# A long convolution factored 256 x 16 or 64 x 64: what the layout of the spectral stages does to the time of a two-head kernel

## The chip, the core and the metric

The kernel runs on one core of a Trainium2 chip. A core has TensorE (PE, with its weight loads as PEld), VectorE (DVE), ScalarE (ACT), GpSimd (POOL) and SyncE (SP), each with an instruction stream of its own that runs in program order, and sixteen DMA engines that move data between HBM and SBUF. SP and POOL issue the DMAs of this kernel: SP on the queue that the profile calls q1, POOL on q0. The metric is the device time of one execution in microseconds; the median of several runs counts. A profile is taken of one execution, and its span goes from the first to the last instruction.

## The reference

Two heads share nothing but the output tensor. With S = 2048 positions and D = 1024 channels:

```python
# head A: short shift filter, gate, long causal convolution by FFT of length 4096, gate
k_shift = sum(k_pad[:, t:t + S, :] * shift_k[:, ks - 1 - t] for t in range(4))
kv = k_shift * v
y  = irfft(rfft(pad(kv, 2 * S)) * rfft(pad(ssm_k, 2 * S)))[:S]
a  = q * (y + kv * ssm_D)
# head B: diagonal complex state space
Lam_bar = exp(dt * Lam);  B_bar = ((Lam_bar - 1) / Lam)[:, None] * Bmat
Bu = einsum("bld,pd->blp", x, B_bar)
h  = scan over t of  Lam_bar * h + Bu[:, t]
b  = 2 * einsum("blp,dp->bld", h, Cmat).real + x * Dskip
out = concatenate([a, b], axis=-1)       # (1, 2048, 2048), bf16
```

## The kernel before

**Head A** computes the length-4096 transform in two factors, N1 = 256 by N2 = 16, with odd frequencies, so that 128 complex values of k1 are enough. Position n is split as n = 16 n1 + n2, n1 on the 128 partitions and n2 from 0 to 15.

- *kv* (L539 to L575): `kp` and `vp` load two n2 rows of k and v for all 128 n1, `kvm`, `kva`, `kvb`, `kvc` build kv for one n2 on DVE.
- *First stage* (L577 to L589): `am` multiplies the kv of one n2 by the 128 x 128 cosine or sine matrix `F1t`, one matmul of 128 x 512 for each of two halves of D and two parts; `ae` evicts the PSUM bank on ACT; `ast` stores 256 KB to the DRAM scratch `Ys_kv` from POOL. `hl`, `hT`, `hc`, `hm`, `he`, `hst` (L591 to L633) do the same for the filter `ssm_k`, after a transpose on PE, into `Ys_h`.
- *Second stage* (L635 to L689), for 16 groups gq of two k1 per partition block: `lh` and `lk` load `Ys_h` and `Ys_kv` again, now with (part, n2, k1 block) on the partitions (512 KB each, SP); `sh` and `sk` multiply by the group's weights `wts` (loaded by `lw`), two matmuls with 64 output rows each that lie in the two halves of one bank; `she` and `ske` evict; `pr` forms the two products on DVE; `sa` transforms back, two matmuls with 64 input rows each into two banks; `sae` evicts and `vst` stores 512 KB to the scratch `Vs`.
- *Third stage* (L691 to L718): `vl` loads both parts of one n2 from `Vs` (two SP loads of 256 KB), `a3` multiplies by `Gt` (two accumulating matmuls of 128 x 512 per half of D), `a3e` evicts, `qm` multiplies by q (loaded by `qp`), `ost` stores to the output from POOL.

There are two barriers in the data: a second-stage group needs all of `Ys_h` and `Ys_kv`, and a third-stage load needs all of `Vs`.

**Head B** fills the engines beside it. For each of 16 chunks of 128 positions: `x` loads x transposed, `U` (L461, 16 matmuls of 128 columns per half step) gives the input projections, `ue` evicts, `r1`, `r2`, `rc`, `sc`, `cm`, `ca`, `r3`, `r4` rotate, scan and rotate back on DVE, `y` (L517) does the output projection, `ye` evicts, `yst` stores. The set-up loads, transposes and tables (`bl`, `bT`, `bc`, `cl`, `cT`, `cc`, `cx`, `tab...`) come first.

**The order.** Everything is issued in the order of one long string, `ORDER`, fixed in the source: each word is a task with its indices, and behind a colon the buffers that it takes (`p` PSUM banks, `a` 4 KB slots, `b` 2 KB slots, `m`, `w`). The framework adds the semaphores that data and buffer reuse need. An engine runs its own instructions in that order, so a DMA on SP or POOL that waits holds up those behind it. `spd` is a DMA issued by SP, `gpd` one issued by POOL.

The lines that matter for a transfer are those that say how DRAM is walked, for instance

```python
kr = k.rearrange("(n s) d -> n s d", s=N2)                                    # 128 x 16 x 1024
Ys.rearrange("c n (s g) d -> (c n s) g d", g=NG)[:, gq * GC:(gq + 1) * GC, :] # l2: 128 x (2 x 1024)
spd(st["vv", n2][:, cc, :], Vs[cc, n2, :, :])                                 # vl: 128 x 1024
```

Of the kernel before, what the change touches and what calls it, by code (L numbers as in the profile page):

```python
# [21 lines left out]
N1, N2, NFFT = 256, 16, 4096  # L22
NG = 32


def a_constants():
    n1 = np.arange(128)[:, None]; k1 = np.arange(128)[None, :]
    ang = 2 * np.pi * n1 * (k1 + 0.5) / N1
    F1 = np.stack([np.cos(ang), -np.sin(ang)], axis=1)
    G = np.stack([np.cos(ang.T) * 2 / NFFT, -np.sin(ang.T) * 2 / NFFT], axis=1)  # L30
    s = np.arange(4)[:, None, None, None]; g = np.arange(NG)[None, :, None, None]
    n2 = np.arange(N2)[None, None, :, None]; k2 = np.arange(N2)[None, None, None, :]
    kk1 = 32 * s + g
    phi = 2 * np.pi * n2 * (2 * kk1 + 1 + 2 * N1 * k2) / (2 * NFFT)
    cph, sph = np.cos(phi), np.sin(phi)
    W2 = np.zeros((2, 4, N2, NG, 2, 4, N2))
    Wa = np.zeros((2, 4, N2, NG, 2, 4, N2))
    Wb = np.zeros((2, 4, N2, NG, 2, 4, N2))
    for si in range(4):
        c_ = cph[si]; s_ = sph[si]  # L40
        c_n2k2 = np.transpose(c_, (1, 0, 2)); s_n2k2 = np.transpose(s_, (1, 0, 2))
        W2[0, si, :, :, 0, si, :] = c_n2k2
        W2[1, si, :, :, 0, si, :] = s_n2k2
        W2[0, si, :, :, 1, si, :] = -s_n2k2
        W2[1, si, :, :, 1, si, :] = c_n2k2
# [12 lines left out]
    Wb = np.transpose(Wb, (0, 1, 2, 3, 4, 6, 5))
    wa = Wa.reshape(2, 64, NG, 128)[0]
    wb = Wb.reshape(2, 64, NG, 128)[0]  # L60
    half = lambda a: np.transpose(a.reshape(64, NG // 2, 2, 128), (2, 0, 1, 3)).reshape(128, NG // 2, 1, 128)
    W3 = np.concatenate([W2.reshape(128, NG // 2, 2, 128), half(wa), half(-wa), half(wb)], axis=2)
    return f(F1), f(G), f(W3)

# [3 lines left out]

ORDER = """
ld_w:a0a1 wb.3:p0 wb.2:p1 wb.0:p2 wb.1:p3 wbe.1 bl.3.1:b0 wb.7:p4 bl.3.0:b1 ld_par par_T:p5 p32 exp1 dve2 exp2 wbe.3 dve3 wbe.2 wb.4:p6 wbe.4  # L70
bl.2.1:b2 bT.2.1:p3 sm_pre bT.3.0:p5 bc.3.0 tabA1:a0a2a3a4 sin0 wbe.7 bl.4.0:b3 bT.4.0:p0 bc.4.0 bl.0.1:b4 bl.2.0:b5 bl.1.0:b6 bT.2.0:p6 wb.5:p5
bc.2.0 bT.3.1:p1 bT.0.1:p4 bl.0.0:b7 bT.0.0:p7 bc.0.0 bc.2.1 sin1 bT.1.0:p0 x.3:b8 U.3.1.0:p3 wb.6:p6 bc.3.1 U.3.1.1 bl.1.1:b9 bT.1.1:p7 bc.0.1 wbe.5
bc.1.0 wbe.6 x.1:b10 U.1.0.0:a1p5 tabA2 wbe.0 U.1.1.0:p0 U.1.1.1 x.2:b2 U.2.1.0:p2 bc.1.1 U.3.0.0:a5p7 ue.3.1 U.2.0.0:a6p3 U.2.0.1 sin2 par_rest eo
kp.1 U.2.1.1 ue.2.1 ue.2.0 z1 kp.0 dd kvm.3:m0 bl.5.0:b0 cl.2.0:b4 bT.5.0:p6 kva.3 kvb.3:b9 bc.5.0 x.0:b5 U.0.0.0:a7p4 U.0.0.1 bl.7.1:b6 U.0.1.0:p3
U.0.1.1 bl.4.1:b7 bT.4.1:p2 U.1.0.1 stt bc.4.1 ue.0.0 kp.-1 bl.5.1:b3 U.3.0.1 ue.3.0 bl.6.0:b1 ue.1.0 kvm.1:m0 cl.2.1:b11 bT.6.0:p2 bT.5.1:p4 bc.5.1
bc.6.0 U.0.2.0:p6 kva.1 kvb.1:b3 z2 cT.2.1:p5 bT.7.1:p7 bc.7.1 bl.6.1:b12 bT.6.1:p4 bc.6.1 kp.-2 kvm.0:m1 kva.0 kvb.0:b12 U.0.2.1 bl.7.0:b13 vp.0:a8
cT.2.0:p2 kvc.1 U.3.2.0:p1 cl.1.0:b14 bT.7.0:p7 U.3.2.1 bc.7.0 vp.1:a9 ue.1.1 ue.0.1 U.1.3.0:p4 U.1.3.1 U.0.3.0:p3 ue.0.2 ue.1.3 kvc.0 ld_F am.0.0:p6
cl.1.1:b0 ae.0.0:b13 U.0.3.1 ue.0.3 kvm.2:m1 cT.1.0:p4 cc.1.0 r1.0:m0 am.0.2:p6 cl.3.1:b7 cT.3.1:p0 x.4:b1 cc.3.1 ae.0.2:b7 cT.1.1:p3 cc.1.1
U.4.0.0:a8p7 cc.2.1 cl.3.0:b11 U.3.3.0:p4 U.3.3.1 ue.3.3 cT.3.0:p6 kva.2 kvb.2:b0 U.4.0.1 kvc.2 ue.4.0 cl.0.0:b6 cT.0.0:p5 cc.0.0 r2.0:a7 cl.0.1:b4
cc.2.0 sc.0.0 am.1.2:p4 am.0.1:p3 U.1.2.0:p0 ae.1.2:b6 U.1.2.1 ae.0.1 cT.0.1:p5 cc.3.0 am.1.3:p2 ast.0.0 sc.0.1 cm.0 ae.1.3 ast.1.1 r3.0:m0 r4.0  # L80
am.0.3:p7 ae.0.3 ast.0.1 U.2.2.0:p4 U.2.2.1 cc.0.1 ue.1.2 am.2.0:p2 r1.1:m1 r2.1:a0 ae.2.0:b12 U.4.3.0:p6 cx.7.0 hl.1.0:a4 U.4.3.1 ue.4.3 hl.0.0:a2
hl.0.1:a3 hT.0.0:p0 hc.0.0:b4 hl.1.1:a10 hT.1.3:p2 hT.1.0:p5 hc.1.0:b13 ld_sd hd.0 am.1.0:p6 ue.3.2 ae.1.0:b6 am.1.1:p7 ae.1.1 am.2.1:p3 ast.1.0
ae.2.1 hd.1 U.2.3.0:p0 hc.1.3:b7 hT.0.2:p5 hc.0.2:b3 U.4.2.0:p1 U.4.2.1 ue.4.2 U.2.3.1 hm.0.0.2:p2 he.0.0.2:b11 x.5:b14 U.5.0.0:a1p3 hm.0.0.3:p1
he.0.0.3 kvc.3 ca.0 rc.1 lw.2:w0 sc.1.0 hm.0.0.0:p5 he.0.0.0:b6 sc.1.1 y.0.0.0:p2 y.0.0.1 U.5.0.1 ast.2.0 hst.0.0.1 cm.1 hm.0.0.1:p5 ue.2.2 ue.2.3
r1.2:m1 hm.0.2.0:p4 cx.5.1 lw.1:w1 hm.1.0.0:p0 he.1.0.0:b4 he.0.0.1 r3.1:m0 am.2.2:p1 ae.2.2:b12 cx.4.1 am.2.3:p7 ae.2.3 y.0.0.2 y.0.0.3 hm.0.2.2:p1
hm.1.0.1:p5 cx.6.0 U.5.3.0:p7 hm.1.3.2:p0 r2.2:a6 ca.1 ast.2.1 he.1.0.1 hst.1.0.0 rc.2 hst.0.0.0 hm.1.0.3:p5 he.0.2.0:b11 hm.0.2.3:p6 hm.0.2.1:p4
he.0.2.2:b0 he.0.2.3 hst.0.2.1 U.5.3.1 r4.1 he.0.2.1 r1.3:m1 ue.5.3 sc.2.0 sc.2.1 cm.2 hT.0.3:p6 ca.2 hm.1.0.2:p4 U.5.2.0:p1 ue.5.0 he.1.3.2:b3
hT.1.2:p3 he.1.0.2:b13 r2.3:a5 rc.3 hm.1.3.0:p0 he.1.3.0:b12 he.1.0.3 hm.1.3.1:p7 he.1.3.1 y.1.0.0:p4 kp.3 hT.1.1:p0 hc.1.1:b4 hst.1.0.1 cx.6.1
hc.0.3:b6 U.5.1.0:p5 U.5.1.1 hm.1.1.3:p0 ue.5.1 cx.4.0 cx.5.0 cx.7.1 y.1.1.0:p7 hm.1.1.2:p5 ye.0.0:b0 hm.1.3.3:p6 he.1.3.3 hst.1.3.1 y.1.0.1
he.1.1.2:b7 he.1.1.3 lw.0:w2 hst.1.1.1 kp.2 kvm.4:m0 hT.0.1:p2 hc.0.1:b13 hc.1.2:b3 y.0.1.0:p6 hm.0.3.2:p0 y.0.1.1 hst.0.2.0 hm.1.1.0:p2 he.1.1.0:b5  # L90
y.0.1.2 hst.1.3.0 y.0.1.3 ye.0.1 hm.0.3.3:p5 he.0.3.2:b7 y.1.0.2 U.5.2.1 y.1.0.3 sc.3.0 ue.5.2 hl.2.1:a9 hm.0.3.0:p2 hm.0.3.1:p6 he.0.3.0:b6 kva.4
hm.1.1.1:p3 he.1.1.1 y.1.1.1 hl.2.0:a4 hT.2.3:p2 hT.2.0:p3 yst.0 he.0.3.3 he.0.3.1 hst.0.3.0 hc.2.0:b12 hm.1.2.3:p5 hm.1.2.2:p1 hst.1.1.0 he.1.2.2:b10
he.1.2.3 r3.2:m1 ye.1.0:b4 y.1.1.2 y.1.1.3 ye.1.1 U.4.1.0:p1 yst.1 U.4.1.1 hc.2.3:b0 hst.1.2.1 hm.0.1.0:p7 sc.3.1 cm.3 hst.0.3.1 ca.3 vp.4:a10 hd.2
hm.2.0.3:p4 hm.2.0.2:p2 hm.2.3.0:p5 he.2.3.0:b11 he.2.0.2:b6 he.2.0.3 hst.2.0.1 hl.3.0:a2 r4.2 y.2.0.0:p3 y.2.0.1 r3.3:m1 r4.3 hm.2.0.0:p2 he.2.0.0:b5
hm.2.3.2:p4 vp.2:a3 kvm.5:m1 hm.1.2.0:p5 hm.2.3.1:p6 he.2.3.1 hm.2.0.1:p0 he.2.0.1 kvb.4:b10 y.2.0.2 he.1.2.0:b12 ue.4.1 y.2.0.3 am.3.0:p0 ae.3.0:b4
kvm.6:m0 kva.6 hst.2.3.0 hm.0.1.1:p5 hm.1.2.1:p6 he.1.2.1 am.3.1:p1 he.0.1.0:b7 he.0.1.1 he.2.3.2:b3 hst.2.0.0 hst.0.1.0 hl.3.1:a7 hT.3.0:p2
y.2.1.0:p0 y.2.1.1 y.2.1.2 hc.3.0:b6 hst.1.2.0 am.3.2:p2 kvc.4 ae.3.1 ast.3.0 ye.2.0:b2 hd.3 hm.0.1.2:p4 hm.2.3.3:p1 hm.0.1.3:p5 he.0.1.2:b11 he.0.1.3
am.3.3:p7 y.2.1.3 am.4.3:p4 am.4.2:p5 ae.4.2:b5 ae.4.3 y.3.0.0:p3 y.3.0.1 ast.4.1 ae.3.2:b9 ae.3.3 ast.3.1 hm.3.0.2:p4 kvb.6:b0 hm.3.0.0:p2 ye.2.1
he.2.3.3 hst.2.3.1 kva.5 am.4.0:p5 ae.4.0:b12 kvb.5:b13 am.4.1:p7 kvc.5 yst.2 vp.3:a0 kvc.6 am.6.2:p6 hst.0.1.1 he.3.0.2:b10 ae.4.1 hm.3.0.3:p0
# [77 lines left out]
ye.14.1 yst.14 a3.7.1:p1 a3e.7.1 ost.11 vl.1:a16 qm.7 ost.7 ost.5 qp.6:a10 a3e.12.0:b12 a3e.12.1 qm.12 ost.12 a3.1.1:p4 a3.1.0:p7 a3.0.1:p2  # L177
a3e.1.0:b13 a3.0.0:p1 a3e.0.0:b0 vl.6:a3 y.15.1.0:p3 a3.6.1:p7 ost.3 a3e.4.1 qm.15 ost.15 qp.0:a14 a3.6.0:p5 qm.4 y.15.1.1 a3.13.1:p6 a3e.6.0:b1
a3e.6.1 y.15.0.0:p5 y.15.0.1 ost.4 y.15.0.2 y.15.0.3 qm.6 ost.6 y.15.1.2 a3e.9.1 qm.9 a3e.1.1 a3e.0.1 qm.0 ost.0 qm.1 ost.1 a3e.13.1 qm.13 ost.13
y.15.1.3 ye.15.0:b12 ost.9 ye.15.1 yst.15  # L180
"""


def full_kernel(ctx, tc, A_q, A_k, A_v, A_shift_k, A_ssm_k, A_ssm_D, B_x, B_Lre, B_Lim, B_Bre, B_Bim,
# [600 lines left out]
```

## Time and profile before

| | |
|---|---|
| median of 3 runs | 389.83 us (389.46 to 393.08) |
| the profiled execution | 391.46 us |
| its span | 389.7 us |
| granted TensorE clock | 0.992 |
| DMA traffic | 92.49 MB, mean 237 GB/s |
| HBM read, written | 52.05 MB, 33.55 MB |
| first stage: `am` L580, `hm` L619 | 64 matmuls of 512 columns, 128 of 256 |
| third stage: `a3` L706 | 64 matmuls of 512 columns |
| `hst` on POOL, L632 | 64 issues, 46.1 us |

How to read it: busy time of PE is the union of its matmuls, which are pipelined, so one that takes 379 ns from start to end may start 216 ns after the one before. A share of the DMA engines is a mean over sixteen. A landing time goes from the issue to the last semaphore update of a transfer, so it includes time in the queue. In the view of stages the columns are the stretch, its length, busy time of each engine with the number of instructions, the granted clock, the DMA share and GB/s.

### The profile page before, as it was taken

The page shows a single profiled execution, that of the slowest core. Times are in us where ns is not written, and L with a number is a line of the kernel's source. Part 1 is how long each engine was busy: PE and PEld are TensorE (multiplying, and loading weights), DVE is VectorE, ACT ScalarE, POOL GpSimd, SP SyncE. Part 2 cuts the span into 40 slices and gives each one's busy share as a digit, 9 for nine tenths or more (in the row PEclk, how much of TensorE's full clock was granted, in tenths as well). Part 3 has the DMA queues.
Part 4 walks back from the last instruction along what each step waited for, and adds up shares of the span by engine and source line. Part 5 has one row for each costly group of instructions (what it writes and reads, how often), then busy time and mean ns, then how long its engine had stood idle before and what let it go on. Part 6 is the DMA issues. An engine that isn't in the chain of part 4 may idle for free.

```text
span 389.7 us, 9237 instructions
## 1 busy us (share of the span) xinstructions
PE 363.3 (93%) x3785; PEld 244.9 (63%) x3785; DVE 332.3 (85%) x335; ACT 278.1 (71%) x519; POOL 93.0 (24%) x156
## 2 busy tenths in 40 slices
PE   4899996999998997999999999999999999999990
PEld 2799995866655866888564556644564656564440
DVE  3899997998899999599999999897897996397760
ACT  3999896767697675869498876887889690345560
POOL 2000022554865652634000002011000320002260
PEclk9999999999999999999999999999999999999996
DMA  8999999676878699586856569748674828879782
GB/s 231 276 301 316 296 181 250 200 228 234 278 205 318 211 238 226 163 274 219 280 204 212 126 208 283 255 145 280 200 275 150 334 109 277 286 252 307 267 319 80
DMA packets 56005, 92.49 MB, mean 237 GB/s; under 512 B 30078, under 2 KB 32126, under 8 KB 55964
## 3 DMA queue, kind: packets, MB, share of 16 engines
q1 hardware_dynamic: 45308, 58.21, 52.9%
q0 software_dynamic: 10656, 33.71, 24.0%
q8 instruction: 29, 0.48, 0.5%
q14 instruction: 12, 0.10, 0.1%
HBM read 52.05 MB, written 33.55 MB: 220 GB/s over the span
## 4 chain that ended last, share of the span: by engine, by line
PE 51%; ACT 14%; issue 12%; DVE 10%; DMA 9%; POOL 2%; POOLq 0%; ACTq 0%; DVEq 0%
PE ps_y L524 18%; PE ps_u L469 15%; PE ps_a L680 4%; PE ps_a L650 4%; DMA Ys_h<-ysbh 4%; ACT hh L657 3%; PE ps_a L619 3%; PE ps_a L580 3%; ACT xx L663 3%; DVE mt L560 2%; DMA Ys_kv<-ysb 2%; ACT vsb L687 2%; DMA out_dram<-ot 2%; DVE mt L567 2%; POOL out_dram L718 1%
## 5 line engine op out<-in xcount | busy, mean ns | idle before, releaser
L524 PE MATMUL ps_y<-CT,h 128*128 128x512 bf16 x512 | 127.0, 379 | 0.3 <-ACT ot L712 0.2
L469 PE MATMUL ps_u<-xT,BT 128*128 128x128 bf16 x2048 | 124.7, 219 | 0.6 <-ACT BT L445 0.3
L469 PEld LDWEIGHTS <-BT 128*128 128x128 bf16 x2048 | 118.4, 98 | 10.5 <-issue 4.1
L524 PEld LDWEIGHTS <-h 128*128 128x128 bf16 x512 | 45.2, 98 | 45.0 <-issue 2.4
L500 DVE TENSOR_TENSOR_SCAN h<-rtab,h 128x1024 bf16<-128x1024 f32 x32 | 71.9, 2279 | 0.3
L471 ACT CAST u<-ps_u 128x512 bf16<-128x512 f32 x64 | 38.6, 628 | 33.0 <-PE ps_u L469 24.4
L632 POOL DMA_DIRECT2D Ys_h<-ysbh x64 | 46.1, 722 | 29.0 <-ACT ysbh L625 23.3
L625 ACT CAST ysbh<-ps_a 128x512 bf16<-128x512 f32 x64 | 35.6, 616 | 16.9 <-PE ps_a L619 6.6
L481 DVE TENSOR_TENSOR mt<-u,Z 128x4096 bf16<-128x4096 bf16 x16 | 36.5, 2281 | 9.6 <-ACT u L471 9.6
L587 ACT CAST ysb<-ps_a 128x512 bf16<-128x512 f32 x64 | 35.5, 630 | 8.2 <-PE ps_a L580 4.1
L689 POOL DMA_DIRECT2D Vs<-vsb x16 | 8.5, 534 | 122.8 <-ACT vsb L687 96.7
L657 ACT CAST hh<-ps_a 128x512 bf16<-128x512 f32 x64 | 36.0, 649 | 2.3 <-PE ps_a L650 2.2
L589 POOL DMA_DIRECT2D Ys_kv<-ysb x32 | 17.5, 551 | 81.4 <-ACT ysb L587 81.4
L481 DVE TENSOR_TENSOR mt<-h,Z 128x4096 bf16<-128x4096 bf16 x16 | 36.6, 2287 | 0.2
L687 ACT CAST vsb<-ps_a 128x512 bf16<-128x512 f32 x64 | 34.2, 694 | 3.3 <-PE ps_a L680 3.3
L663 ACT CAST xx<-ps_a 128x512 bf16<-128x512 f32 x64 | 35.8, 660 | 0.6 <-PE ps_a L650 0.6
L535 ACT CAST yo<-ps_y 128x512 bf16<-128x512 f32 x32 | 19.5, 626 | 16.4 <-PE ps_y L524 16.3
L560 DVE TENSOR_TENSOR mt<-kring,wbc 128x4096 bf16<-128x4096 bf16 (+3 forms) x16 | 30.1, 1884 | 0.1
L529 PE MATMUL ps_y<-Dd,xT 128*128 128x128 bf16 x128 | 28.0, 219 | 0.0
L619 PE MATMUL ps_a<-hT,F1t 128*128 128x256 bf16 x128 | 20.5, 272 | 5.6 <-ACT hT L607 3.6
L712 ACT CAST ot<-ps_a 128x512 bf16<-128x512 f32 x32 | 17.4, 606 | 10.7 <-PE ps_a L706 6.3
L670 DVE TENSOR_TENSOR pp<-xx,hh 128x2048 bf16<-128x2048 bf16 x16 | 19.4, 1220 | 6.0 <-ACT xx L663 3.5
(110 smaller groups left out, 460.3 us busy)
## 6 DMA issues: line engine op xcount, KB each, us to landing
Ys_kv<-ysb POOLq DMA_DIRECT2D x32, 256.0 KB, 3.6
Ys_h<-ysbh POOLq DMA_DIRECT2D x64, 128.0 KB, 3.5
l2h<-Ys_h SPq DMA_DIRECT2D x16, 512.0 KB, 5.7
l2k<-Ys_kv SPq DMA_DIRECT2D x16, 512.0 KB, 4.6
Vs<-vsb POOLq DMA_DIRECT2D x16, 512.0 KB, 5.4
vv<-Vs SPq DMA_DIRECT2D x32, 256.0 KB, 4.9
kring<-in_A_k_dram SPq DMA_DIRECT2D x8, 512.0 KB, 4.3
v<-in_A_v_dram SPq DMA_DIRECT2D x8, 512.0 KB, 5.9
```

The lines of the kernel that those rows point to most:

```text
L469: nc.tensor.matmul(pu[:, w, jl, :], BT[:, 2 * jp + jl, w, d, :], xT[:, d, :], start=(d == 0), stop=(d == ND - 1))
L471: E["ue"] = lambda i, jp: nc.scalar.copy(st["u", i][:, :, 2 * jp:2 * jp + 2, :], st["pu", i, jp][:])
L481: nc.vector.tensor_mul(m, s_, win(Z))
L500: nc.vector.tensor_tensor_scan(gf, rt1, gf, 0.0, ALU.mult, ALU.add)
L524: nc.tensor.matmul(py[:], h[:, 1 - w, j, :], CT[:, j, w, dh * 512:(dh + 1) * 512], start=(j == 0 and w == 0), stop=(j == NJ - 1 and w == 1))
L560: nc.vector.tensor_mul(m[:, 0:h0, :], kring[:, s0:s0 + h0, :], wbc[:, 0:h0, :])
L587: nc.scalar.copy(st["ysb", n2, cc][:, dh * 512:(dh + 1) * 512], st["pa", n2, w][:])
L625: nc.scalar.copy(st["yh", qd, n4, w // 2][:, :, w % 2, :], st["pa", qd, n4, w][:].rearrange("p (c d) -> p c d", c=2))
L632: gpd(Ys_h[cc, n0:n0 + 2, :, qd * DQ:(qd + 1) * DQ].rearrange("n k d -> k n d"), t_[:, cc, :, :])
L657: nc.scalar.copy(st["hh", gq][:, cc, w * 512:(w + 1) * 512], st["ps", "l2h", gq, cc, w][:])
L663: nc.scalar.copy(st["xx", gq, cc][:, w * 512:(w + 1) * 512], st["ps", "l2k", gq, cc, w][:])
L687: nc.scalar.copy(st["vsb", gq][:, gi, w * 512:(w + 1) * 512], st["ps", "v", gq, w][gi][:])
```

## The change

The transform is factored N1 = 64 by N2 = 64 instead of 256 by 16, so that 32 complex values of k1 (HK) are enough. Position n is now split as n = 64 n1 + 16 q + s, with q from 0 to 3 and s from 0 to 15 (NB): a tile of k, v or q has (q, n1) on its 128 partitions.

- The first kv stage needs matrices of 32 x 64 (`F1t`), the last one of 64 x 32 (`Gt`). A new helper `pieces` places eight such matmuls at different rows and columns of the array, each with 512 columns, into four banks (`am`, for two s at once) or two banks (`a3`, for two n2 at once).
- The filter's first stage uses a block-diagonal matrix `Fht` of the full 128 x 128, one matmul of 512 columns in place of two of 256; `hst` becomes one store of 256 KB in place of two of 128 KB.
- The second stage keeps its matmuls and evictions, with dense weights. `l2` issues two loads of 256 KB per tensor and group in place of one of 512 KB.
- The scratch tensors change their layout, and with them every DRAM pattern of `ast`, `hst`, `l2`, `vst` and `vl`; k, v, q and the output of head A are walked as `q n s d`.
- Twelve stores, nine `ost` and three `yst`, are issued by SP instead of POOL.
- `ORDER` is a new string with new slots; the constants get one more load (`ld_H`).

```diff
-N1, N2, NFFT = 256, 16, 4096
-NG = 32
+N1, N2, NFFT = 64, 64, 4096
+HK = N1 // 2
+NB = 16
...
+SP_STORES = frozenset("ost.0 ost.4 ost.5 ost.6 ost.7 ost.8 ost.9 ost.12 ost.13 yst.11 yst.12 yst.15".split())
+    stq = lambda kind, n: spd if "%s.%d" % (kind, n) in SP_STORES else gpd
...
-    Ys_kv = tc.dram_tile([2, N2, P, D], BF16, name="Ys_kv")
-    Ys_h = tc.dram_tile([2, N2, P, D], BF16, name="Ys_h")
-    Vs = tc.dram_tile([2, N2, P, D], BF16, name="Vs")
-    kr = k.rearrange("(n s) d -> n s d", s=N2)
...
+    Ys_kv = tc.dram_tile([4, HK, 2, NB, D], BF16, name="Ys_kv")
+    Ys_h = tc.dram_tile([4, HK, 2, NB, D], BF16, name="Ys_h")
+    Vs = tc.dram_tile([HK, 2, N2, D], BF16, name="Vs")
+    kr, vr, qr, oar = (a_.rearrange("(n q s) d -> q n s d", q=4, s=NB) for a_ in (k, v, q, out_a))
...
     def kp(r):
         if r >= 0:
-            spd(t_, kr[:, 2 * r:2 * r + 2, :])
+            spd(t_, kr[:, :, 2 * r:2 * r + 2, :])
         else:
-            spd(t_[1:113, :, :], kr[0:112, N2 + 2 * r:N2 + 2 * r + 2, :])
-            spd(t_[113:P, :, :], kr[112:P - 1, N2 + 2 * r:N2 + 2 * r + 2, :])
+            rows = slice(NB + 2 * r, NB + 2 * r + 2)
+            spd(t_[32:P, :, :], kr[0:3, :, rows, :])
+            spd(t_[1:32, :, :], kr[3, 0:31, rows, :])
...
+    def pieces(banks, rows, weights, cols):
+        m = weights.shape[-1]
+        for r, pt in enumerate(banks):
+            rs = slice(rows * r, rows * r + rows)
+            for j in range(P // m):
+                nc.tensor.matmul(pt[m * j:m * j + m, :], weights[rs, :], cols(j, r)[rs], start=True, stop=True)
+
+    def am(u, w):
+        st["pa", u, w] = [ptile("ps_a", [P, 512]) for _ in range(4)]
+        pieces(st["pa", u, w], 32, F1t[:], lambda j, r: st["kv", 2 * u + j][:, w * 512:(w + 1) * 512])
...
+    def ast(u, r):
+        gpd(Ys_kv[r, :, :, 2 * u:2 * u + 2, :].rearrange("k c t d -> t (k c) d"), st["ysb", u, r][:])
...
     def hm(qd, n4, w):
-        for cc in range(2):
-            nc.tensor.matmul(pt[:, cc * DQ:(cc + 1) * DQ], F1t[:, cc, :], st["hT", qd, n4][:, w, :], start=True, stop=True)
+        nc.tensor.matmul(pt[:], Fht[:, qp_, :], st["hT", qd, n4][:, 2 * tp:2 * tp + 2, :].rearrange("p a b -> p (a b)"), start=True, stop=True)
...
+    def hst(qd, n4, qp_):
+        dst = Ys_h.rearrange("(b q) k c t d -> b (q k c) t d", b=2)
+        gpd(dst[qp_, :, 4 * n4:4 * n4 + 4, qd * DQ:(qd + 1) * DQ], st["yh", qd, n4, qp_][:])
...
     def l2(nm, Ys, gq):
-        spd(st[nm, gq][:], Ys.rearrange("c n (s g) d -> (c n s) g d", g=NG)[:, gq * GC:(gq + 1) * GC, :])
+        for gi in range(GC):
+            spd(st[nm, gq][:, gi, :], Ys[:, gq * GC + gi, :, :, :].rearrange("q c t d -> q (c t) d"))
...
+    E["vst"] = lambda gq: gpd(Vs[gq * GC:(gq + 1) * GC].rearrange("g c n d -> (c n) g d"), st["vsb", gq][:])
+
+    def vl(u, h):
+        st["vv", u, h] = k4("vv", [P, 2, D])
+        src = Vs.rearrange("k c (q t) d -> t (k c) q d", q=4)
+        for a in range(2):
+            spd(st["vv", u, h][:, a, :], src[2 * u:2 * u + 2, :, 2 * h + a, :])
...
+    def a3_(u, w):
+        st["po", u, w] = [ptile("ps_a", [P, 512]) for _ in range(2)]
+        pieces(st["po", u, w], 64, Gt[:], lambda j, r: st["vv", u, j // 2][:, j % 2, w * 512:(w + 1) * 512])
...
-    E["ost"] = lambda n2: gpd(oar[:, n2, :], st["ot", n2][:])
+    E["ost"] = lambda n2: stq("ost", n2)(oar[:, :, n2, :], st["ot", n2][:])
```

## The prediction

> **What bounds the kernel now.** I read the page's part 1 first, then busy time by stage. The stages are cut where the trace cuts them: the last store of Ys_kv starts at 183.2 us and the first load of l2k at 187.0; the last store of Vs starts at 320.4 and the first load of vv, which needs every Vs store, at 323.6.
>
> ```profile
> PE 363.3 (93%) x3785; PEld 244.9 (63%) x3785; DVE 332.3 (85%) x335; ACT 278.1 (71%) x519; POOL 93.0 (24%) x156
> ```
> ```profile
> core 0: us, PE busy (x) PEld busy (x) DVE busy (x) ACT busy (x) POOL busy (x), PEclk, DMA share, GB/s
> 0.00:185.00 185.00, 169.72 (x2113) 136.22 (x2115) 165.79 (x199) 143.50 (x254) 69.49 (x112) 1.00 0.87 244
> 185.00:317.00 132.00, 131.03 (x1214) 73.85 (x1213) 122.50 (x97) 106.19 (x213) 10.09 (x19) 1.00 0.66 218
> 317.00:381.00 64.00, 62.58 (x464) 34.85 (x459) 44.03 (x41) 28.43 (x55) 12.89 (x25) 1.00 0.81 283
> 381.00:390.00 9.00, 0.00 (x0) 0.00 (x0) 0.00 (x0) 0.00 (x0) 0.54 (x1) 0.64 0.11 43
> ```
>
> PE is busy 131.0 of 132 us in stage B and 62.6 of 64 in stage C; in A and B DVE is nearly as full. PE and DVE set the pace, and transfers are hidden. But the DMA share, a mean over 16 engines, is already 0.66 to 0.87: there is no room for a transfer that uses few of the sixteen. So the last views are the DMA issues and the landings (the first landing line is that of vv, the second of l2k).
>
> ```profile
> DMA packets 56005, 92.49 MB, mean 237 GB/s; under 512 B 30078, under 2 KB 32126, under 8 KB 55964
> q1 hardware_dynamic: 45308, 58.21, 52.9%
> q0 software_dynamic: 10656, 33.71, 24.0%
> l2h<-Ys_h SPq DMA_DIRECT2D x16, 512.0 KB, 5.7
> l2k<-Ys_kv SPq DMA_DIRECT2D x16, 512.0 KB, 4.6
> vv<-Vs SPq DMA_DIRECT2D x32, 256.0 KB, 4.9
> ```
> ```profile
> DMA to landing us min/median/max: 2.6/4.9/5.6
> DMA to landing us min/median/max: 3.4/4.6/7.9
> ```
>
> **The compute side of the change.** Three answers price it: the timeline of PE around old two-piece stages and around `a3`.
>
> ```profile
> 229.63 0.59 PE L680 MATMUL ps_a<-pp,wts 64*128 64x512 bf16 x4
> 230.06 0.60 PE L680 MATMUL ps_a<-hh,wts 64*128 64x512 bf16 x4
> 368.08 3.62 PE L706 MATMUL ps_a<-vv,Gt 128*128 128x512 bf16 x16
> ```
>
> Sixteen whole-array matmuls take 3.62 us; less the latency of one (0.38), 15 steps of 0.216. Four half-array ones start 0.43 us before the next four: two run beside each other. At 207.85 an L524 follows four L680 that start at 207.31, 0.54 later and not 0.43: a change of array shape costs 0.1 us.
>
> - `am` and `a3`: 128 matmuls of 0.216 (27.6 us) become 32 groups of eight. Eight at once: 0.216 and up to two shape changes, 0.22 to 0.42 a group, 7 to 13 us, a gain of 15 to 21. One after another: 256 x 0.216 = 55.3, a loss of 28. I take 17 gained, by the nearest row (two pieces do run beside each other).
> - `hm`: 128 of 256 columns become 64 of 512, the same columns: nothing. Evictions stay 128x512 in the same number: nothing on ACT. DVE's work is unchanged.
> - POOL: `hst` falls from 64 to 32 issues, 46.1 us of POOL busy to perhaps 30. POOL is 24% busy: nothing. SP gets 32 more l2 issues and 12 stores, 44 x 0.38 = 17 us; it mostly waits. A store on SP waits for `qm` or `ye`, and behind it wait the `vl` and `qp` loads, 0 to 2 us each late in stage C; I count nothing, since the transfers' own time below is longer.
> - Tail: POOL's drain at L780 starts at 381.2 with the last store and takes 7.65 us; the span ends at 389.7. After, POOL's last stores are `yst.14` and `ost.11`, before `yst.15` is done; 0 to 4 us gained.
> - Order and slots: counts per engine and stage stay, apart from some U and y moved into stage C; 5 us either way.
>
> Alone these give about 389.7 - 17 - 2 = 371, bounded by DVE's 332 us of work and some 17 of start and tail (349).
>
> **The transfers.** Every large copy of before has 128 rows as outermost count on both sides. The change permutes DRAM: `kr, vr, qr, oar` read "q n s d", counts 4 x 32 x row; l2 reads `q (c t) d`, 4 x 32 x 1,024; `vl` reads `t (k c) d`, 2 x 64 x 1,024. The two `kp` loads with negative index become 3 x 32 rows and 31 rows.
>
> How a copy is cut over engines can be read from the trace's packet records. Each engine that takes part in a copy on q1 ends with a 4-byte packet. There are 144 plain copies and 24 transposing ones (32 such packets each, 768). If all used sixteen engines there would be 3,072; there are 3,038. The 34 missing are exactly 4 x 8 for the parameter loads of 8 rows and 2 x 1 for the `kring` loads of 15 rows. So a copy is divided over as many engines, up to sixteen, as its outermost count gives. q0 (POOL) posts sixteen for each of its 149 copies, and shows nothing of this. I extend the row to the new shapes: 4 engines for kp, vp, qp, l2 and `ost` on SP, 2 for `vl`, 3 and 1 for the odd `kp`, always the first ones, since no record shows a rotation. That is the step that carries the forecast.
>
> The Trainium skill says the same against this change: "DMA: Bandwidth & Descriptors", section "Why a DMA increments its semaphore by 16 and not by 1", has the issuer take the largest number up to 16 that divides the slowest dimension of both sides, on hardware queues the lowest-numbered engines. By it the sum stays as below; the trace agrees in the 34 packets, and no run yet shows it for a pattern that is 4 or 2 on the DRAM side alone.
>
> What one engine moves: in the records a 2,048-byte packet on q1 takes 84 ns (median), 24.4 GB/s. Ends: vv against l2k, 256 KB more cost 0.8 us on sixteen engines, 20.5 GB/s each; a 4,096-byte packet at 156 ns at least is 26.3 GB/s. I take 84 ns, since the new loads are rows of 2 KB.
>
> Load of engine 0, by stage:
> - A: 16 kp and vp of 512 KB, 64 packets of 2 KB each: 1,024 x 84 ns = 86 us. Odd kp: 2 x (64 + 62) x 84 = 21. The rest stays spread: 0.87 x 185 = 161, less the old k and v (9.4 MB / 16 / 24.4 = 24) = 137. Together 244; but packets overlap (the share reaches 1.13 in 10 to 40 us), and at 26 GB/s it is some 195. Between: 210.
> - B: 64 l2 loads x 32 x 84 ns = 172. Rest: 0.66 x 132 = 87, less old l2 (16.8 MB / 16 / 24.4 = 43) = 44. Three `qp`: 16. Three early `lh` fall in A: -16. Sum 216; with a few idle us at the start of the stage 220.
> - C: `vl` 32 x 64 x 84 ns = 172. All of them come after the last Vs store. Five `qp` 27, nine `ost` on SP 24, rest about 15: 238.
> - Tail 8.
>
> 210 + 220 + 238 + 8 = **676 us** of span. The profiled execution took 391.46, 1.8 beyond its span, and the median of the runs is 1.6 below it; the two cancel, and I say 675. PE's gain vanishes: in C it has some 50 us of work (9 half-U of 0.9, 40 y parts of about 0.92, a3 5).
>
> Stores on POOL with counts 2 and 4 (`ast`, seven `ost`): if they too sat on the first engines, `ast` would add 172 us to A; spread, nothing. I take nothing, since q0 posts on all sixteen.
>
> Ends: at 20.5 GB/s A 245, B 268, C 284, together with the tail 800; at 26.3 GB/s 190, 195, 208, together 600. A mixed case decides the range's ends, 590 to 790.
>
> **Rivals.**
> 1. *The SBUF side's 128 partitions decide the cut* (faster). Then all sixteen engines serve, vv lands in 3 to 5 us as now, and the compute sum holds: about 372. It decides from seven engines up: the `vl` loads take 344/k us on k engines, and at k = 7 they pass under stage C's 50 us of PE work. For it: only copies that are short on both sides show fewer engines so far. Against: nothing in the rows says that one side is exempt. 0.10.
> 2. *Few engines, but others each time.* Bytes spread; only landing grows, for vl 1.9 + 64 x 84 ns = 7.3 us. Prefetch hides most: 372 to 395, say 385. 0.05.
> 3. *The pieces run one after another* with loads as in 1: 389.7 + 28 - 2 of tail = about 416, as PE has no idle time to take it in. Against: the pairs above. 0.03.
>
> **How the numbers follow.** Forecast 0.82, range 590 to 790 nearly all of it, so close to 0.8 in all. Faster by over 1%: rival 1 and part of 2, 0.12; within 1% 0.01; slower 0.87. One per cent is about what a measurement of this kernel can tell from no change.
>
> **What would show it.** Right: stage C some 240 us long with traffic near 75 GB/s in place of 283; vv to landing tens of us, and `a3` waiting for DMA vv; fewer q1 packets of 4 bytes than copies times sixteen; in B, L650 waiting for l2h and l2k. The pieces: eight L706-like starts within some 0.1 us. Wrong: vv landing near 5 us and PE still over 90% busy. The forecast also fails in size if an engine moves far more than 26 GB/s, or if PE's clock falls in the waits so far that compute matters again.

## The result, and the profile after

The changed kernel takes **729.57 us** (725.6 to 730.67, four runs) against 391.01 us (389.46 to 393.08, four runs) of the kernel before, timed beside it: 1.863 times as long, interval 1.851 to 1.876. The profiled execution took 730.67 us, 2.0 us beyond its span of 728.7. Ratios here and below leave out executions more than 1.5% above the fastest of their kernel; three of the seven of the kernel before that were timed with the later versions were such.

The first view is the page's part 1 and 2 of the changed kernel: busy time by engine, and the clock in 40 slices.

```profile
PE 420.2 (58%) x3849; PEld 259.2 (36%) x3849; DVE 330.3 (45%) x335; ACT 282.1 (39%) x519; POOL 78.2 (11%) x113
...
PEclk9969879978798677979778887799556555855685
```

No engine is near full any more: PE had 93% before and DVE 85%. DVE's time in us is that of before, so the work has not grown. PE's own 420.2 in place of 363.3 comes with a granted clock of 0.768 on average, against 0.992 before.

The second view is the busy time by stage of the changed kernel, cut at its first load of l2k (284.4 us), its first load of vv (502.7) and just behind its last store. The columns are the stretch, its length, busy time of each engine with the number of instructions, the granted clock, the DMA share and GB/s.

```profile
core 0: us, PE busy (x) PEld busy (x) DVE busy (x) ACT busy (x) POOL busy (x), PEclk, DMA share, GB/s
0.00:284.00 284.00, 189.98 (x2132) 145.61 (x2133) 166.29 (x200) 148.47 (x260) 56.53 (x81) 0.83 0.75 161
284.00:502.00 218.00, 157.34 (x1272) 81.68 (x1270) 123.48 (x98) 109.05 (x212) 14.96 (x22) 0.84 0.55 139
502.00:717.00 215.00, 72.84 (x453) 31.94 (x450) 40.50 (x38) 24.56 (x48) 6.67 (x10) 0.64 0.20 71
717.00:729.00 12.00, 0.00 (x0) 0.00 (x0) 0.00 (x0) 0.00 (x0) 0.00 (x0) 0.50 0.25 84
```

The stages A, B and C last 284, 218 and 226 us, against 187, 137 and 66 before (from the start to the first load of l2k, to the first load of vv, to the end). In C the traffic is 71 GB/s in place of 283, and PE works a third of the time. The DMA share of 0.20 is a mean over sixteen engines; three full ones give 0.19.

Third, the chain that ended last, by engine and by line, from the page of the changed kernel:

```profile
DMA 47%; PE 22%; SPq 19%; ACT 5%; issue 3%; POOL 1%; DVE 1%; ACTq 0%; POOLq 0%
SPq L686 12%; DMA vv<-Vs 12%; DMA Ys_kv<-ysb 11%; DMA l2k<-Ys_kv 10%; PE ps_y L505 8%; DMA wts<-a_c_W 6%; PE ps_u L450 5%; SPq L633 3%; PE ps_a L641 3%; DMA ld<-in_B_B_im_dram 3%; DMA Vs<-vsb 2%; PE ps_a L671 2%; DMA xT<-in_B_x_dram 2%; SPq L420 1%; ACT ysb L575 1%
```

Transfers and SP's queue hold two thirds of it. `SPq L686` is SP itself at the issue of `vl`: the next view, the changed kernel's instructions of line 686, gives min, median and max in ns of such an issue, and the first and last start. Before it was 319/403/1470.

```profile
L686 SPq DMA_DIRECT2D vv<-Vs x32: 520/5086/8511, 502.7 to 669.3; - x32
```

The median of 5.09 us is near 64 packets of 84 ns, 5.4 us: in the steady state an issue lasts as long as one load's packets on each of its two engines. Everything behind it in SP's order stands still as long. That shows in the waits of the changed kernel (total us, times, longest):

```profile
PE ps_a L565 <- DMA vv<-Vs: 130.3, 22, 21.9
...
DVE ot L706 <- DMA qt<-in_A_q_dram: 90.0, 2, 58.4
...
PE ps_a L641 <- DMA wts<-a_c_W: 46.5, 7, 10.4
...
DVE acc L555 <- DMA Ys_kv<-ysb: 37.2, 3, 24.1
...
ACT ysbh L617 <- DMA Ys_kv<-ysb: 30.3, 3, 10.5
```

The `wts` loads are copies of 128 whole rows, which the change did not touch. They are late for two reasons. They stand behind the cut copies in SP's order, and once issued they land late: the changed kernel's chain has, as its longest step of this kind (start, length, what),

```profile
259.67 17.32 DMA wts<-a_c_W
```

where such a load of the kernel before landed after 3.4 us (median). The packet records show why. Of the 128 packets of 1,280 bytes of this load, 96 start 3.5 to 4.7 us after the issue, and the other 32, the share of four engines in sixteen, only after 15.3 to 16.8. So a copy that is spread over all sixteen engines still waits for the four that hold the cut copies.

Two counts of packet records complete the picture. On q1 the changed kernel leaves 2,076 packets of 4 bytes. That is what the prediction's cut gives: 64 l2 x 4, 32 vl x 2, 24 of k, v and q x 4, the odd k loads 2 x 3 + 2 x 1, 9 `ost` x 4, 51 untouched copies x 16, four parameter loads x 8, and 768 of the transposing ones. On q0 there are 15,680 packets of 8 bytes that before had none of: 32 `ast` x 14 x 32, and 7 `ost` x 12 x 16. So POOL's stores are cut in the same way, over 2 and 4 engines, and each idle engine gets one small filler packet for every data packet that a working one carries. The 16 posts on q0, which the prediction read, did not show this: they are still 1,696 in the changed kernel, sixteen for each of its 106 copies.

The pieces do run beside each other, as the timeline of PE around an `am` shows (start, length, instruction, count):

```profile
236.81 0.33 PE L450 MATMUL ps_u<-xT,BT 128*128 128x128 bf16 x3
237.07 0.42 PE L565 MATMUL ps_a<-acc,F1t 32*64 32x512 bf16 x8
237.42 0.57 PE L450 MATMUL ps_u<-xT,BT 128*128 128x128 bf16 x7
```

The eight matmuls of 512 columns start within 0.023 us of each other and are over in 0.42 us; a single one takes 0.38.

### The profile page after: what moved, and what is told of

The parts are those of the page before. It is cut to its first block, busy times and chain, and to the rows that moved or that the text cites. A ratio compares the mean times of both kernels' runs of the same rounds, so it can differ in the third digit from the quotient of the medians.

```text
span 728.7 us, 9352 instructions
## 1 busy us (share of the span) xinstructions
PE 420.2 (58%) x3849; PEld 259.2 (36%) x3849; DVE 330.3 (45%) x335; ACT 282.1 (39%) x519; POOL 78.2 (11%) x113
## 4 chain that ended last, share of the span: by engine, by line
DMA 47%; PE 22%; SPq 19%; ACT 5%; issue 3%; POOL 1%; DVE 1%; ACTq 0%; POOLq 0%
SPq L686 12%; DMA vv<-Vs 12%; DMA Ys_kv<-ysb 11%; DMA l2k<-Ys_kv 10%; PE ps_y L505 8%; DMA wts<-a_c_W 6%; PE ps_u L450 5%; SPq L633 3%; PE ps_a L641 3%; DMA ld<-in_B_B_im_dram 3%; DMA Vs<-vsb 2%; PE ps_a L671 2%; DMA xT<-in_B_x_dram 2%; SPq L420 1%; ACT ysb L575 1%
## 5 line engine op out<-in xcount | busy, mean ns | idle before, releaser
L450 PE MATMUL ps_u<-xT,BT 128*128 128x128 bf16 x2048 | 140.8, 236 | 10.5 <-DMA xT<-in_B_x_dram 4.8
L450 PEld LDWEIGHTS <-BT 128*128 128x128 bf16 x2048 | 134.8, 107 | 32.1 <-issue 24.2
L505 PE MATMUL ps_y<-CT,h 128*128 128x512 bf16 x512 | 141.2, 413 | 0.5 <-ACT ysbh L617 0.4
L565 PE MATMUL ps_a<-vv,Gt 64*32 64x512 bf16 x128 | 17.4, 598 | 130.3 <-DMA vv<-Vs 130.3
L706 DVE TENSOR_TENSOR ot<-ot,qt 128x1024 bf16<-128x1024 bf16 x16 | 10.2, 687 | 115.1 <-DMA qt<-in_A_q_dram 90.0
L565 PEld LDWEIGHTS <-Gt 64*32 64x32 bf16 x128 | 3.2, 99 | 141.4 <-issue 140.5
L641 PEld LDWEIGHTS <-wts 128*64 128x64 bf16 x256 | 16.6, 131 | 95.9 <-DMA wts<-a_c_W 50.3
L641 PE MATMUL ps_a<-l2k,wts 128*64 128x512 bf16 x128 | 29.8, 484 | 35.0 <-DMA l2k<-Ys_kv 20.9
L641 PE MATMUL ps_a<-l2h,wts 128*64 128x512 bf16 x128 | 27.7, 512 | 35.3 <-DMA wts<-a_c_W 33.9
L579 POOL DMA_DIRECT2D Ys_kv<-ysb x32 | 25.8, 810 | 113.4 <-ACT ysb L575 113.3
```

Of the source, the lines that this page charges most:

```text
L450: nc.tensor.matmul(pu[:, w, jl, :], BT[:, 2 * jp + jl, w, d, :], xT[:, d, :], start=(d == 0), stop=(d == ND - 1))
L505: nc.tensor.matmul(py[:], h[:, 1 - w, j, :], CT[:, j, w, dh * 512:(dh + 1) * 512], start=(j == 0 and w == 0), stop=(j == NJ - 1 and w == 1))
L641: nc.tensor.matmul(pt[64 * gi:64 * gi + 64, :], st["w", gq][:, gi, 64 * cc:64 * cc + 64], st[nm, gq][:, gi, w * 512:(w + 1) * 512], start= ...
```

## The experiments

The theory under test: each copy is cut over as many engines as its outermost count, and this alone makes the changed kernel slow. Against it stand the new order, the pieces, and rows that lie scattered in DRAM. The first four undo the cut for one kind of copy each, and then for all: the same bytes and rows, in one copy for each outermost index. Each is one execution, and the kernel before took 392.92 us on that chip.

**The loads of `vl` alone.**

```diff
-        for a in range(2):
-            spd(st["vv", u, h][:, a, :], src[2 * u:2 * u + 2, :, 2 * h + a, :])
+        for t in range(2):
+            spd(st["vv", u, h][64 * t:64 * t + 64, :, :], src[2 * u + t, :, 2 * h:2 * h + 2, :])
```

> Only vl changes: each of its 32 loads of 256 KB now takes the 64 rows (k, c) of one t for two n2, outermost count 64 instead of 2; the same rows of 2 KB, 128 KB apart, arrive in the same tile. Theory (few engines): a load is spread over 16 engines, the 172 us on engines 0 and 1 become 21, stage C falls from 227 us to 90 to 110 (qp and ost still on four engines, 50 us of PE work at a lower clock), the whole to 600 to 625 us. Rival (the rows lie far apart in DRAM, the cut does not matter): stage C stays, 720 to 735 us. Rival (order or pieces): 720 to 735 us.

Measured: 597.94 us, 131.6 less and 2 us below the range; C lasts 96 us, inside its own. The first line is the vv issue and its span of time, the others are waits, of this kernel:

```profile
L686 SPq DMA_DIRECT2D vv<-Vs x32: 573/574/1553, 499.8 to 548.2; - x32
```
```profile
DVE ot L706 <- DMA qt<-in_A_q_dram: 17.2, 2, 9.0
...
PE ps_a L565 <- DMA vv<-Vs: 14.3, 10, 6.7
```

The loads need 48 us in place of 167, SP is free after 0.57 us, and the wait for `qt`, which nobody edited, falls from 90.0 to 17.2: it had come from `vl`. In the changed kernel the last three `qp` loads are issued only at 602.2, 673.0 and 680.2, behind `vl` in SP's order, and DVE still waits until 622.3 and 694.8, 15 to 22 us after the issue. A and B stay as they were (500 against 503 us to the first load of vv).

**The loads of `l2` alone.**

```diff
-        for gi in range(GC):
-            spd(st[nm, gq][:, gi, :], Ys[:, gq * GC + gi, :, :, :].rearrange("q c t d -> q (c t) d"))
+        for qq in range(4):
+            spd(st[nm, gq][32 * qq:32 * qq + 32, :, :], Ys[qq, gq * GC:(gq + 1) * GC, :, :, :].rearrange("g c t d -> (c t) g d"))
```

> Only lh and lk change: four loads of 128 KB per tensor and group, one for each q, outermost count 32 instead of 4; the same rows, twice as many issues on SP. Theory (few engines): the 172 us on four engines in stage B become 43, stage B falls from 218 us to 140 to 160, the whole to 650 to 675 us. Rival (rows apart, or order): 720 to 735 us; with 64 more issues of 0.4 us on SP up to 750.

Measured: 653.42 us, 76 less, inside the theory's range. The first load of vv starts at 425.3 in place of 502.7, and PE's wait for `wts` falls from 46.5 to 5.4 us.

**The stores of the kv spectrum, `ast`, alone.**

```diff
-        gpd(Ys_kv[r, :, :, 2 * u:2 * u + 2, :].rearrange("k c t d -> t (k c) d"), st["ysb", u, r][:])
+        for t in range(2):
+            gpd(Ys_kv[r, :, :, 2 * u + t, :].rearrange("k c d -> (k c) d"), st["ysb", u, r][64 * t:64 * t + 64, :])
```

> Only ast changes: two stores of 128 KB from POOL, one for each t, outermost count 64 instead of 2, in place of one of 256 KB; the same rows, 32 KB apart. Theory, with the step that the prediction left out (POOL's stores are cut in the same way, and two engines take 15 us for each): landing falls from 15 to 4 to 6 us, stage A from 284 to 225 to 245 us, the whole to 670 to 690. Rival (stage A is long because kp, vp and the loads queued behind them wait for four engines): landing falls, but the whole stays over 715.

Measured: 696.67 us, 33 less, 6.7 short of the range. The stores land after 6.7 us (median) in place of 15.0, and the first load of l2k comes at 248.5 in place of 284.4.

**All of them**, with k, v, q and `ost` in one copy for each quarter as well, and the odd k loads in pieces of 32, 32, 32, 16 and 15 rows.

> All of it: vl, l2, ast as before in this study, and kp, vp, qp and ost cut into one copy for each q (outermost count 32; the odd kp 16 and 15). The same rows everywhere, more issues (SP some 130 more, POOL some 50 more). Theory (few engines is the whole loss): 365 to 400 us, vv landing under 8 us, PE busy over 85% in all stages. Rival (rows apart): over 600. Rival (order, slots or pieces are worse by themselves): 420 to 500 with transfers landing early and PE waiting for DVE or ACT.

Measured: 375.46 us, half of the changed kernel. The same kernel, timed again:

> The version with every copy cut over all the engines (one load or store per outermost index) timed against the kernel before. The compute sum of the prediction, without its transfers, gave 371. Theory (nothing but the cut of the copies holds the changed kernel back): 371 to 378, 3 to 5% faster than before. Rival (its first time of 375.46 was a chance of one execution, and order or the SP queue eat the gain): 385 to 393.

372.46 us (370.07 to 374.74, four runs) against 389.91 (median of seven): a ratio of 0.958, interval 0.950 to 0.966. Page and stages of this run (cut at the last store of Ys_kv, the last store of Vs, and near PE's end):

```profile
PE 351.6 (95%) x3849; PEld 229.7 (62%) x3849; DVE 328.4 (88%) x335; ACT 278.3 (75%) x519; POOL 94.3 (25%) x166
```
```profile
0.00:172.00 172.00, 163.70 (x2102) 126.36 (x2103) 161.97 (x199) 145.28 (x258) 63.63 (x113) 1.00 0.97 261
172.00:300.00 128.00, 127.77 (x1178) 69.86 (x1176) 119.39 (x93) 106.34 (x212) 15.12 (x23) 1.00 0.83 240
300.00:364.00 64.00, 59.64 (x576) 33.45 (x574) 47.00 (x45) 26.10 (x50) 15.51 (x31) 0.95 0.94 250
```

PE is full again and the clock back. Nothing but the cut of the copies held the changed kernel back: order, slots, pieces and late stores are all still in.

**The loads of k and v alone**, in the changed kernel:

```diff
-            spd(t_, kr[:, :, 2 * r:2 * r + 2, :])
+            for qq in range(4):
+                spd(t_[32 * qq:32 * qq + 32, :, :], kr[qq, :, 2 * r:2 * r + 2, :])
...
-        spd(st["v", r][:], vr[:, :, 2 * r:2 * r + 2, :])
+        for qq in range(4):
+            spd(st["v", r][32 * qq:32 * qq + 32, :, :], vr[qq, :, 2 * r:2 * r + 2, :])
```

> The changed kernel with only the loads of k and v cut by hand: one copy per quarter in place of one of 128 rows with outermost count 4, the two odd ones in pieces of 32, 32, 32, 16 and 15 rows. Theory (A's length is the sum on the first engines: 107 us of k and v, some 103 of the rest, and the stores of the first kv stage's spectrum, 172 us of packets on POOL's two engines): A loses up to the 107 us, as long as the spectrum stores, which alone need 172 us plus their share of the rest, don't hold it: A ends near 230 to 260 in place of 284, total 675 to 705. Rival 1 (the k and v loads are not what A waits for; only the spectrum stores are): 720 to 735. Rival 2 (the spectrum stores lie on engines of their own and cost A nothing): A near 185 to 200, total 630 to 650.

Measured: 689.57 us, 40 less, inside the theory's range. A ends at 243.7, 41 earlier. So cutting k and v alone takes 41 us from A and cutting the spectrum's stores alone 36; with every copy cut A is 284.4 - 169.6 = 115 shorter. Cutting `l2` alone had brought its first load of l2k to 274.5, 10 earlier, as such a load then needs one quarter of the spectrum only. The other 28 go only when the copies are cut together: each hides a part of the other.

**Is it the outermost count, or the scattered rows?** In the kernel before, only the source of `vl` is walked in another order, once with outermost count 2 and once with 64:

```diff
-            spd(st["vv", n2][:, cc, :], Vs[cc, n2, :, :])
+            spd(st["vv", n2][:, cc, :], Vs[cc, n2, :, :].rearrange("(a b) d -> b a d", b=2))
```
```diff
-            spd(st["vv", n2][:, cc, :], Vs[cc, n2, :, :])
+            spd(st["vv", n2][:, cc, :], Vs[cc, n2, :, :].rearrange("(b a) d -> a b d", b=2))
```

> The kernel before, in which only the 32 loads of the third stage's input are changed: the same 256 KB in rows of 2 KB, but read in the order even rows, odd rows, so that the outermost count in DRAM is 2 (the rows of the spectrum are permuted by it, so the output differs). Theory (a copy is cut over as many engines as its outermost count): two engines move 32 x 64 packets of 2 KB at 84 ns, 172 us after the last spectrum store at about 322 us, and the end comes at 505 to 535. Rival (the order of the rows in DRAM, or the SBUF side's 128 partitions, decide): 388 to 400, as the control.

> The control to the one before: the kernel before with the same loads, again in permuted rows of 2 KB (rows i and i+64 by turns, so that the spectrum's rows are permuted and the output differs), but with outermost count 64. Theory (only the outermost count matters): 385 to 400, unchanged. Rival (rows of 2 KB out of order are what costs): 500 or more, as the one before.

Measured: 536.58 and 400.34 us; the kernel before took 394.77 beside them. Of each, first the one with 2, the page's row of q1 and the issue of the loads:

```profile
q1 hardware_dynamic: 44860, 58.21, 37.6%
```
```profile
L694 SPq DMA_DIRECT2D vv<-Vs x32: 493/5222/7396, 326.8 to 489.6; - x32
```

and the one with 64:

```profile
q1 hardware_dynamic: 45308, 58.21, 51.8%
```
```profile
L694 SPq DMA_DIRECT2D vv<-Vs x32: 512/604/1375, 329.4 to 368.6; - x32
```

The control has exactly the 45,308 packets of the kernel before; the other has 448 fewer, which is 32 loads x 14 engines that take no part. This one pattern in an otherwise unchanged kernel costs 142 us, 1.6 above the range; PE's clock falls to between 0.5 and 0.9 in that stage too. The control is 0.3 above its range and 5.6 above the kernel before, one execution of each; single executions of the kernel before lie between 386 and 396 us, so that the order of the rows costs little or nothing.

**Where do POOL's cut copies lie?** To the kernel with outermost count 2 the same was done on its 16 output stores, all on POOL:

```diff
-    E["ost"] = lambda n2: gpd(oar[:, n2, :], st["ot", n2][:])
+    E["ost"] = lambda n2: gpd(oar[:, n2, :].rearrange("(a b) d -> b a d", b=2), st["ot", n2][:])
```

> The kernel before with the 32 loads of the third stage's input at outermost count 2 (which gave 536.6), and now its 16 output stores on POOL too: the same 256 KB each, written in the order even rows, odd rows, outermost count 2 (rows of the output are permuted by it, so it differs). Question: do POOL's copies of count 2 lie on the same two engines as SP's? A store then is 64 packets of 2 KB on each of two engines, 5.4 us, 16 of them 86 us; the loads keep their two engines busy from 327 to about 515. Theory (the same two, the first): the stores' packets queue up with the loads' and the end comes 50 to 86 us later, 585 to 625. Rival (others): 16 stores of 5.4 us fit beside the loads, and only the last ones show: 535 to 550.

Measured: 536.84 us, unchanged, inside the rival's range. The issue of DMAs in this kernel: the stores land after a median of 14.2 us in place of 5.7.

```profile
out_dram<-ot POOLq DMA_DIRECT2D x16, 256.0 KB, 14.2
```

The 7,168 fillers on q0 (16 x 14 x 32) say that the stores are cut over two engines, and yet the total shows nothing taken from the two that the loads fill. Nor is it another fixed pair: the last five stores, issued from 515.6 to 519.4, are all landed by 533.4, 1.31 MB in 17.9 us or 73 GB/s, and two engines at 4,096 bytes in 159 ns make 51.5.

**The term that the prediction took as nothing, alone**: the version with all copies cut, with `ast` uncut again.

> As the version with every copy cut (372.5), but the store of the first kv stage's spectrum is again one copy of 256 KB with outermost count 2, on POOL: the term that the prediction took as nothing, alone. In the version where only the k and v loads are cut, each such store lands 9 to 18 us after its issue, and four issued within 3.4 us land within 6.8 us, less than the 5.1 us apiece (32 packets of 4 KB at 159 ns) that one pair of engines would need: so different copies lie on different engines. Theory (the cost is the landing: some 10 us more for each store until its slot is free again, with 32 stores on the way of the slots that the filter's stores use too): the stage until the last of these stores grows from 172 us to 195 to 240, total 395 to 440. Rival 1 (POOL's pieces rotate and prefetch hides the landing): 370 to 380. Rival 2 (all on one pair of engines): at least 41 + 32 x 5.1 = 204 to the last store plus its landing, and the other POOL stores behind it, 410 to 450.

Measured: 441.64 us, 69 more than the 372.5, 1.6 above the theory's range and inside rival 2's. The stores land after 14.4 us (median). The issue and first and last start of the stores, and three waits of this kernel:

```profile
L583 POOL DMA_DIRECT2D Ys_kv<-ysb x32: 796/798/847, 41.8 to 230.6; - x32
```
```profile
ACT ysb L579 <- DMA Ys_kv<-ysb: 17.2, 4, 10.7
ACT ysbh L621 <- DMA Ys_kv<-ysb: 16.0, 2, 9.1
DVE acc L559 <- DMA Ys_kv<-ysb: 15.3, 2, 13.8
```

The last such store starts 59 us later than in the version with all copies cut (171.9). The total alone would not rule out rival 2, one fixed pair; the rate does: the last nine stores, issued from 218.4 on, are landed at 249.1, 2.36 MB in 30.7 us or 77 GB/s, above the 51.5 of two engines. What a single store costs shows in the packet records of the second one, in a stretch where little else runs: two engines, on each a packet of 4 KB every 0.311 us, though the packet itself takes 0.159. That makes 32 x 0.311 = 10 us for a store. It was issued at 43.7 and landed at 57.2; a store of the same size over all engines lands in 3.6 (median, the kernel before). Why an engine spends half of that time between packets, these records don't show. That the landing makes up the 69 us through the slots, which `ysb`, `ysbh` and `acc` wait for, fits the waits shown, but ACT's add up to 33 of the 69, and DVE's may overlap with them; the rest was not told apart.

**One `ost` for each row group again**, in the version with all copies cut: nine stores of outermost count 4 on SP and seven on POOL.

```diff
-    def ost(n2):
-        for qq in range(4):
-            stq("ost", n2)(oar[qq, :, n2, :], st["ot", n2][32 * qq:32 * qq + 32, :])
+    E["ost"] = lambda n2: stq("ost", n2)(oar[:, :, n2, :], st["ot", n2][:])
```

> As the version with every copy cut, but each output row group is stored again with one copy whose outermost count is 4 (9 stores on SP, 7 on POOL, in place of 64). Theory A (the tail of the cut version is held by some 36 store issues on SP of about 0.47 us each, which end 3 to 4 us after the last eviction): 371 to 373, 2 to 4 us less. Theory B (nine stores of 256 KB on engines 0 to 3, 32 packets of 2 KB or 2.7 us of an engine each, pile up at the end): 376 to 382, no gain or a loss.

Measured: 393.55 us (391.03 to 396.71), 1.015 of before, interval 1.004 to 1.026: 21 us more than with 64 stores, beyond what either theory gave, on the side of B. The timeline of SP at the end:

```profile
356.78 19.08 SPq L714 DMA_DIRECT2D out_dram<-ot  x9
375.97 2.24 SPq L518 DMA_DIRECT2D out_dram<-yo  x1
```

The 19 us are not a sum of nine issues: waits lie between them, and the 36 issues of the version with 64 stores span 20.2 us as well. But an issue now lasts up to 3.1 us (0.55 with 64 stores), and the final store behind them starts at 376.0 in place of 367.9 and takes 2.2 us in place of 0.4. The two profiled executions differ by 18.1 us. Behind PE's last matmul lie 17.7 us in place of 6.6, so 11.1 of the 18.1 are this tail. PE's last matmul ends 7.1 later; 3.5 of that are there at the first load of vv, before any `ost`, and the rest was not told apart. Sixteen copies in the wrong shape thus undo the whole gain.

**The first kv stage in whole-array matmuls again**, in the version with all copies cut. Its constant is block-diagonal, and its store is one of 128 rows.

```diff
-        pieces(st["pa", u, w], 32, F1t[:], lambda j, r: st["kv", 2 * u + j][:, w * 512:(w + 1) * 512])
+        for r, pt in enumerate(st["pa", u, w]):
+            nc.tensor.matmul(pt[:], F1t[:, r % 2, :], st["kv", 2 * u + r // 2][:, w * 512:(w + 1) * 512], start=True, stop=True)
```

> As the version with every copy cut, but the first kv stage runs as whole-array matmuls again: its constant becomes a 128x256 block-diagonal of the four copies, 64 matmuls of 128x128 on 512 columns take the place of 128 of 32x64, and the stage's store is one copy of 128 rows. Theory (the pieces are worth what the prediction put on them, and PE sets the pace): the stage's PE time goes from some 16 groups of 0.3 to 0.4 us to 64 x 0.216 = 13.8 us, 7 to 9 us more; with PE busy over 90% of the span, 382 to 386. Rival (DVE or the loads set the pace in the stage before the first spectrum is stored, where this work lies, and the pieces buy nothing there): 373 to 378.

Measured: 376.51 us (375.55 to 377.57), 4.0 more than with pieces, below the theory's range and inside the rival's. The ratios to before, 0.969 (0.962 to 0.975) and 0.958 (0.950 to 0.966), have intervals that overlap, though each of the four runs lies above each of the four with pieces, timed beside them. The groups of PE, first with pieces and then whole:

```profile
L569 PE MATMUL ps_a<-acc,F1t 32*64 32x512 bf16 x128 | 7.5, 395 | 1.5 <-ACT ysb L579 0.7 <-DVE acc L561 0.7
```
```profile
L575 PE MATMUL ps_a<-acc,F1t 128*128 128x512 bf16 x64 | 16.1, 379 | 0.0
```

PE's time in the stage differs by 8.6 us, as expected; about half of it arrives in the total. This speaks against PE alone setting the pace there: the stage lies in A, where DVE is nearly as full. The whole version also issues half the stores, which was not separated.

## Why the prediction was right, and where its sum was not

**The mechanism held.** The outermost count on the DRAM side decides the cut, though SBUF has 128 partitions on the other side: the 2,076 packets and the pair of edits in the kernel before show it, the 448 missing packets to the unit. Rival 1 (the SBUF side decides) is out. Its time of 372, the compute sum, is what came out once the copies were cut by hand: 372.5. Rival 2 (few engines that rotate) is out for SP, whose copies pile up on the same engines (an issue of `vl` every 5.09 us, and the 32 late packets of `wts`); on POOL that is what happens. Rival 3 is out by the eight starts within 23 ns.

**By stages.** A: 210 said, 284 measured. B: 220 and 218. C with the tail: 246 and 226. The sum came out at 676 against a span of 728.7, by a miss of 74 in A that 20 too many in C made smaller.

**The step that failed is the one on POOL's stores**: "spread, nothing. I take nothing, since q0 posts on all sixteen". The posts are made by all engines even when two move the data: sixteen for each copy, beside 14 x 32 fillers for each `ast`. That the engines of SP stay free of it was right, and so the 172 us that the prediction named as the other end were not due either; but each store then takes 10 us or more to land, and what waits for its slot pays. With `ast` cut, A ends 36 us earlier; the other 38 of the 74 lie in the sum for k, v and the rest: A then still takes 248.5, close to the 244 that the prediction had worked out from the records before it took 210 for overlap. The split depends on what else is cut: put back alone into the version with all copies cut, the same stores move their last start by 59 us. The Trainium skill has in "DMA: Bandwidth & Descriptors", section "Why a DMA increments its semaphore by 16 and not by 1", that on SP's kind of queue the lowest engines serve, and on POOL's kind a run of neighbours from a cursor that goes round. The trace agrees in the 77 GB/s above, more than one fixed pair moves. So `ast` loads no engine much, and its price had to be read from the landing of one store.

**B and C.** 84 ns for a packet of 2 KB was the right row: 5.09 us of an SP issue is 64 packets at 80 ns. Of the eight `qp` loads five were issued before C, the first at 424.8, where the prediction had three; two less in C are 11 of the 20 that it had too many.

**SP's queue.** To count nothing for SP failed as a step, though the sum did not need it: the two or four engines behind it set the same pace. An issue that lasts as long as a transfer holds back what stands behind it (`qt`, `wts`), and the full engines hold it back again once it is issued. The version with all copies cut has many more issues on SP, of its plain copies none longer than 2.1 us (8.5 in the changed kernel), and PE no longer waits for `wts`.

**The compute side.** 371 was said without the transfers, and 372.5 measured. Inside it, PE's rows for `am` and `a3` fall from 20.1 + 16.3 to 7.5 + 7.1 us, 21.8 less; 17 was said, from 15 to 21, counted in steps of 0.216 where these rows are unions with the latency in them. Of `am`'s part only 4 us reached the total when it was tried alone. PE's last matmul ends 9.3 us before the end of the span in the kernel before, and 6.7 in the version with all copies cut: 2.6 of the tail, 2 was said. The rest of the 17.4 gained was not taken apart; `a3` and the order remain for it. That the total met the sum so closely is therefore not shown to come from the terms of the sum, and may be luck in part.

**The clock** was named as a way to go wrong: it fell to 0.64 in C, where PE waits most.

## What to carry to other kernels

Before a change of layout, write down the outermost count of every DMA pattern on both sides. Where it is below sixteen, split the copy by that index into several with a long outermost count. A count above sixteen is no guarantee: each of the two loads of 31 rows of k was served by one engine (2 x 1 in the count of packets above), and the versions with k cut split it into 16 and 15. More issues of half a microsecond each are cheap beside one that holds two engines and its issuer. A mean DMA share far below one can be a few engines at their limit: look at how long an issue lasts and at the small packets that each engine leaves. For a queue where every engine posts, count the fillers, read one copy's landing alone, and look for what waits for its slots.

The version that came out of it, the change with all its copies split, takes 0.958 of the kernel before.

## What the runs showed of the hardware beyond that

- POOL's copies over two engines run on changing pairs (77 and 73 GB/s where a fixed pair makes 51.5); one of 256 KB takes about 10 us alone, a packet of 4 KB every 0.311 us on each engine, where the packet lasts 0.159 us. On SP's queue a packet of 2 KB takes 84 ns (median).
- A copy over all sixteen engines lands with the slowest of them: of a `wts` load in the changed kernel a quarter of the packets start 12 us after the rest.
- An SP issue can last as long as the packets of one copy on its few engines: 5.09 us (median) with 64 packets of 2 KB an engine, up to 3.1 us with 32 (`ost`, at the end of the version with `ost` uncut), and 0.57 us where the copy goes over all sixteen.
- The packets of 256 bytes of the transposing loads, which the change did not touch, took 72 ns on average in the changed kernel and 26 in the version with all copies cut, the median 18 in both. What they wait for was not looked into.
- A change of array shape cost PE about 0.1 us: in the version with all copies cut, the next whole-array matmul starts 0.331 us after the last of eight pieces of `am`, and the first piece of `a3` 0.309 us after a whole-array one (medians), where whole-array ones of 512 columns follow each other in 0.216. The Trainium skill's "TensorEngine Tiling (Array Packing)", section "Key Properties", has a change of mode drain the array and gives no time for it; the trace agrees in these 0.1 us.
